# Ten of forty unpacking steps of the first float64 weight chunks, moved from the attention to the routing rounds and behind the branch

## The chip, the cores and the metric

One core of a Trainium2 chip runs the whole program as one launch. The metric is the device time of one execution in microseconds (us): the span from the program's first to its last instruction, and a little around it.

## The reference, cut to what matters

```python
# 1. attention: 2 x 8 heads, 768 positions, head size 64, window 128, 4 sink positions
scores = q @ k.T / sqrt(D);  scores[~(is_sink | in_window)] = -1e9
x = softmax(scores) @ v                      # -> (1536, 512), float32
# 2. routing: every token goes to one of 8 experts, at most 192 tokens to each
logits = x @ w_gate
for idx in argsort(-logits.flatten()):       # greedy, best pair first
    if assigned[tok] < 0 and counts[e] < cap: assigned[tok] = e; counts[e] += 1
# 3. experts: out[mask] = relu(x[mask] @ w1[e]) @ w2[e]
# 4. dense block: h = x @ w_in;  (h * sigmoid(h)) @ w_out
```

`w_in` and `w_out` reach the kernel as float64 (a float32 array times a float64 scalar). All other arrays are float32.

## The kernel before

The work runs in four stages, one after the other, since each needs what the last one leaves.

**Attention** (`attention_band`). The twelve tiles of 128 queries by eight heads give 96 steps `n`, and a loop written out by hand issues all engines' work step by step. At each fourth `n` TensorE makes the scores of four heads (`s_mm`, L271). VectorE takes the merge (`s_merge`, L291) and the masked minimum with its read-out (`s_max`, L299) for each head. ScalarE takes the exponentials two steps later (`s_exp`, L308). TensorE transposes them five steps later (`tr`, L322) and multiplies them with the values thirteen steps later (`pv`, L369, L371, L374). The PSUM pool `s` has four banks, and `s_mm` needs two of them, so it waits until the minima of earlier heads have been read. `hooks[n]` is a list of functions that are called at the top of step `n`, ahead of that step's merge and minimum.

**Unpacking** (`Weights.unpack`). A float64 chunk is loaded as raw 32-bit words into one of seven `raw` buffers (512 KB each) and turned into float32 in `f`. A chunk is four such pieces, and each piece takes five steps: s0 (for the first two chunks ScalarE, an absolute value, L969), s1 (VectorE, clamp, L975), s2 (VectorE, shift and mask, L979), s3 and s4 (VectorE, each combining `raw` and `f`, L983 and L987). Step s4 gives the raw buffer back and issues the load of the next piece. The first two float64 chunks are eight pieces, so forty steps; `unpacked` issues the next one. They are used only in the dense stage.

**Routing** (`Route`). Rounds of threshold tests and counts: VectorE compares (L675 to L692), VectorE and ScalarE build the grids `G` (L710, L715), TensorE counts (L723), VectorE turns the counts into `sel` (L732), TensorE adds it up (L733). Two rounds run over a part of the tiles at the end of the attention (`plan`), four full rounds after it (`run`, `iterate`). `iterate` calls the parts of a round in order: steps, ScalarE's grids, VectorE's grids, counts, rise (`sel` and L733). `between(k)` lets the weights' work run on beside the rounds: ScalarE rounds a float32 piece of an expert's weights (L1014), GpSimd takes the remainder (L1017). Then `finish` makes the row numbers `idx` (L897) and a flag, and a branch on the flag (L778) leads past more rounds that these inputs do not need. GpSimd gathers the first expert pair's rows with three indirect DMAs (L1155).

**Experts and dense block.** TensorE transposes the gathered rows (L1197), ScalarE rounds them (L1211), VectorE takes the remainder (L1212), and the products begin (L1238). All later unpacking is woven between the products.

The `quiet` memsets (L344) are one-element writes on VectorE, 59 of them ahead of the first step.

Of the kernel before, what the change touches and what calls it, by code (L numbers as in the profile page):

```python
# [184 lines left out]
HH = H // 2  # L185
LT, LP, LS = 5, 13, 6
LATE = 9, 10
QUIET = 59
VWS = {8: [((0, (0,)), 0)], 10: [((0, (0,)), 1)], 11: [((0,), 2)], 13: [((0, (1,)), 0)], 16: [((0, (1,)), 1)],
       58: [((1,), 2)]}  # L190
for m in range(1, NT // 2):
# [5 lines left out]
def attention_band(tc, qd, kd, va_d, vt_d, vs_d, sel_d, wbd_d, eye_d, n_sink, ident, x_d, L_sb, pp, hooks={}):  # L197
    nc = tc.nc
    with ExitStack() as ctx:
# [21 lines left out]
        def load_va(i):  # L221
            if i < NT:
                nc.sync.dma_start(va[:, i % NB], va_d[i // NB, i % NB])
# [79 lines left out]
        def s_exp(n):  # L303
            i, h = divmod(n, H)
            if h == 0:
                A[i] = wp.tile([P, H, KW], F32, name="A", bufs=3)
            t, nm = TS.pop(n)
            nc.scalar.activation(A[i][:, h], t, AF.Exp, bias=nm, scale=-1.0)  # L308
            if h == H - 1:
                a = wp.tile([P, 3, H, 4], F32R, name="a96")  # L310
                src = A[i][:, :, 0:4]
                nc.gpsimd.tensor_copy(a[:, 0], src)
                nc.gpsimd.tensor_copy(a[:, 2], src)
                nc.gpsimd.tensor_tensor(a[:, 1], src, a[:, 0].bitcast(F32), OP.subtract)
                A[i, "s"] = a
# [26 lines left out]
        quiet = cp.tile([1, 1], F32, name="quiet")  # L342
        for _ in range(QUIET):
            nc.vector.memset(quiet, 0.0)  # L344
# [3 lines left out]
        def warm(k):  # L348
            for _ in range(k):
                for sl in map(slice, WE, WE[1:]):  # L350
                    nc.tensor.matmul(idle[:, sl], zero[:, :P], zero[:, sl], start=True, stop=True)
# [108 lines left out]
        def feed(*qs):  # L460
            for q in qs:
                if q:
                    f = q.popleft()
                    if f:
                        f()
                    return
# [5 lines left out]
        for n in range(NH + LP + 5):  # L472
            i, h = divmod(n, H)
            now[0] = n
            dve_now.extend(at_step.pop(n, ()))
            if n < NH and n % 4 == 0:
                s_mm(n)
            if n < len(WARM) - 1:
                warm(WARM[n + 1])
            for f in hooks.get(n, ()):  # L480
                if f is None:
                    while dve_now:
                        feed(dve_now)
                else:
                    f()
            if 0 <= n - 2 < NH:
                s_exp(n - 2)
            if 0 <= n - LT < NH:
                tr(n - LT)
            feed(act_now, act_bg)  # L490
            if n < NH and n % 2 == 0:
                s_merge(n)
                s_merge(n + 1)
            feed(dve_now, dve_bg)
            if n < NH:
                s_max(n)
            feed(dve_now, dve_bg)
            feed(act_now, act_bg)
            for _ in range(3 if n >= NH + LT and n - NH not in LATE else 0):
                feed(act_late)  # L500
            it, ht = divmod(n - LS, H)
            if ht == H - 1 and 0 <= it < NT:
                sink_tr(it)
            if n < NH and h == 0:
                if i == 4:
                    nc.sync.dma_start(vsf[1][:96], vs_d[:96, 1])
                if i % 2 == 0:
                    load_vt(i + 2)
                    load_vt(i + 3)
                if i + 3 < NT:  # L510
                    load(i + 3)
                load_va(i + 2)
            for at, f in VWS.get(n, ()):
                (vw, vw_tr, sinks)[f](*at)
            if 0 <= n - LP < NH:
                pv(n - LP)
# [16 lines left out]
NA, RP = 4, 6  # L533
RS, AT = 256.0, (None, 8, None, 9, None, 10, None, 11)
HOT, HOLD = 4, (12, 10, 5, 4)
# [27 lines left out]
class Route:  # L563
# [170 lines left out]
        ]  # L734
        return steps, [partial(grid_act, t) for t in range(na)], grids, counts, rise

    def iterate(self, na, warm=0):
        g = self.G
        parts = self.iteration(NT, na)
        self.warm(warm if g is not None else 0, g)  # L740
        for part in parts:
            for s in part:
                s()

# [4 lines left out]
            s()  # L749
        return oh  # L750

    def run(self, L, idx, nit, more, bg=lambda k: None, speculate=lambda: None):
        self.place(self.psum("s"))
        for k in range(nit):
            bg(k)
            if k + 2 == nit:
                self.foresee("settled")
            self.iterate(NA, HOLD[0] if k == 0 else 0)
            self.warm(HOLD[1 + (k + 1 == nit)])
            if k == 0:  # L760
                self.scaled()
        bg(nit)
        badi = self.result(idx)
        speculate()
        self.warm(HOLD[3])
        self.further(badi, L, idx, more, speculate, "settled")
# [152 lines left out]
SPIN, REST = (2, 2), 9  # L919
MIX, AHEAD = (1, 1, 0), 3  # L920
PLAIN, MIXED = "uuddduuddd", "ududududududu"
FIRST, EVEN, ODD = (17, 25, 33, 45, 53, 60, 67), (40, 46, 52, 58, 64, 70, 76, 80, 84, 88), range(33, 93, 2)


class Weights:
# [631 lines left out]
NIT, MORE, SN = 4, (2, 6), -9  # L1557
# [4 lines left out]
def fused(tc, a, out, n_sink, window):  # L1562
    nc = tc.nc
    with ExitStack() as ctx:
        ctx.enter_context(tc.manual_schedule())
        cp = ctx.enter_context(tc.tile_pool(name="consts", bufs=1))
        dp = ctx.enter_context(tc.tile_pool(name="dram", bufs=1, space=DRAM))
        ident = cp.tile([P, P], F32, name="ident")
        make_identity(nc, ident)
        L = cp.tile([P, NT, E], F32, name="L")  # L1570
        idx = cp.tile([P, E // 2, 3], I32, name="idx")
        x_d = dp.tile([B * S, DM], F32, name="x_d")
        sums_d = dp.tile([NT, P, DM], F32, name="sums_d")
        mix_d = dp.tile([2, P, 3, 4 * 2 * CAP], F32, name="mix_d")
        def load_route():
            route.load(a["offs"], a["dlts"])

        order, mixed = weight_order(a["w1"], a["w2"], a["wi"], a["wo"])
        raws = ctx.enter_context(tc.tile_pool(name="raws", bufs=1, reuse_waits="tile"))
        f64 = ctx.enter_context(tc.tile_pool(name="f64s", bufs=1, reuse_waits="tile"))  # L1580
        W = Weights(tc, raws, f64, order, 4, 7, 4, mixed)
        rest = ExitStack()
        with rest:
            rp = rest.enter_context(tc.tile_pool(name="r_w", bufs=2, side="right"))
            rc = rest.enter_context(tc.tile_pool(name="r_c", bufs=1, side="right"))
            route = Route(tc, rc, ident)
            if banded(n_sink, window):
                pp = rest.enter_context(tc.tile_pool(name="p", bufs=1, space=PSUM))
                hooks = {NT * H // 2: [load_route]}
                for n in FIRST:  # L1590
                    hooks.setdefault(n, []).append(W.load)
                for n in sorted({*EVEN, *ODD}):
                    hooks.setdefault(n, []).append(W.unpacked)
                plan(route, rp, lambda n: pp.tile([P, 512], F32, name=n, bufs=PB[n]), L, hooks)
                attention_band(tc, *(a[k] for k in ("qd", "kd", "va", "vt", "vs", "sel", "wbd", "eye")), n_sink,
                               ident, x_d, L, pp, hooks)
                W.unpack_all()
                route.values(L, NT - 1, NT)
            else:
                load_route()  # L1600
                W.fetch()
                W.unpack_all()
                attention(tc, *(a[k] for k in ("qd", "kd", "vd", "wg")), n_sink, window, ident, x_d, L)
                pp = rest.enter_context(tc.tile_pool(name="p", bufs=1, space=PSUM))
                route.open(rp, lambda n: pp.tile([P, 512], F32, name=n, bufs=PB[n]))
                for s in route.scale(L, NT):
                    s()
                route.begin()
                route.values(L, 0, NT)
            fp = ctx.enter_context(tc.tile_pool(name="ffn", bufs=1, reuse_waits="tile"))  # L1610
            W.start(fp)
            rows = Rows(tc, x_d, idx)
            def between(k):
                if k == NIT:
                    rows.quiet()
                else:
                    W.preload(4, PRE[k])

            route.run(L, idx, NIT, MORE, between, lambda: rows.gather(0))
        W.preload(4)  # L1620
        silu = cp.tile([P, 1], F32, name="silu")
        nc.scalar.activation(silu, ident[:, 0:1], AF.Silu)
        ffn(tc, rows, idx, ident, W, out, sums_d, mix_d)
# [115 lines left out]
```

## Time and profile before

| | us |
|---|---|
| runs | 546.32, 547.36, 548.28 (median 547.36) |
| profiled execution, time | 547.26 |
| profiled execution, span | 545.5 |
| attention, to TensorE's last value product | about 97 |
| full rounds and row numbers, to `idx` | about 122 |
| first product of the experts (L1238) | 128.61 |
| experts to dense block | about 281 |

Times in a profile are counted from the span's start. The profiled execution stands 0.1 us below the median of the runs, and its time is 1.8 us longer than its span.

### The profile page before, as it was taken

How to read it: one execution, taken by the hardware profiler on the slowest of the kernel's cores; microseconds unless marked ns; L12 is line 12 of the kernel's file. 1: busy time of each engine (PE TensorE's matmuls, PEld its weight loads, DVE VectorE, ACT ScalarE, POOL GpSimd, SP SyncE). 2: the span in 40 equal slices, each digit the busy share in tenths (PEclk: the TensorE clock that was granted, in tenths of full speed). 3: DMA queues.
4: the chain of work that ended last, by engine and by line, in shares of the span. 5: the costliest groups of instructions: out<-in, count | busy, mean ns of one | idle time of the engine just before them, and what ended most of it. 6: DMA issues, size and time to landing. Idle time of an engine off the chain costs nothing.

```text
span 545.5 us, 10811 instructions
## 1 busy us (share of the span) xinstructions
PE 526.4 (96%) x3937; PEld 482.4 (88%) x3937; DVE 345.4 (63%) x991; ACT 301.6 (55%) x611; POOL 243.7 (45%) x251
## 2 busy tenths in 40 slices
PE   7999899789999999999999999999999999999995
PEld 6898798667999999999999898998888899888984
DVE  5677898772443453444338998768979877853523
ACT  4677676655776786777644554543554344443330
POOL 4567565377899999999991000000000000000304
PEclk9999999899999999999999999999999999999999
DMA  7989972256466666666640654453677656276503
GB/s 210 381 282 319 316 265 73 76 196 182 143 210 222 223 229 217 226 228 222 225 150 1 258 186 177 172 191 102 220 262 245 234 181 224 99 225 223 194 12 117
DMA packets 43941, 108.00 MB, mean 198 GB/s; under 512 B 4650, under 2 KB 12458, under 8 KB 43884
## 3 DMA queue, kind: packets, MB, share of 16 engines
q1 hardware_dynamic: 41696, 100.88, 54.3%
q0 software_dynamic: 1920, 6.29, 3.4%
q8 instruction: 32, 0.52, 0.4%
q14 instruction: 25, 0.20, 0.1%
q10 hardware_dynamic: 268, 0.10, 0.1%
HBM read 86.81 MB, written 20.45 MB: 197 GB/s over the span
## 4 chain that ended last, share of the span: by engine, by line
PE 69%; issue 4%; POOL 2%; DMA 1%; ACT 0%; DVE 0%; POOLq 0%; another core or an unknown queue 0%; DVEq 0%; ACTq 0%
PE h L1332 21%; PE acc L1454 21%; PE mm L1238 9%; PE m L1261 8%; PE mm L1241 4%; PE m L1264 4%; POOL out L1425 2%; PE mm L1261 1%; PE mm L1197 1%; DMA row<-x_d,idx 1%; PE mm L1264 1%; PE m L1238 0%; POOLq L1735 0%; PE m L1197 0%; ACT wr L1014 0%
## 5 line engine op out<-in xcount | busy, mean ns | idle before, releaser
L1017 POOL TENSOR_TENSOR wr<-raw,wr 128x1024 fp32r<-128x1024 f32 x64 | 150.7, 2390 | 8.2 <-ACT wr L1014 8.1
L1454 PE MATMUL acc<-wr,gt 128*128 128x512 f32 x576 | 145.4, 395 | 0.0
L1454 PEld LDWEIGHTS acc<-wr,gt 128*128 128x128 f32 x576 | 107.3, 188 | 19.4
L1425 POOL DMA_INDIRECT out<-raw,idx x12 | 11.6, 964 | 241.5 <-DVE raw L1466 241.3
L1332 PE MATMUL h<-x,wr 128*128 128x384 f32 x528 | 101.3, 339 | 0.0
L1332 PEld LDWEIGHTS h<-x,wr 128*128 128x128 f32 x528 | 93.8, 188 | 4.0 <-DVE keep L1366 0.3
L1238 PE MATMUL mm<-xg,wr 128*128 128x384 f32 x248 | 72.4, 360 | 0.5 <-DVE xg L1212 0.3
L1014 ACT ACTIVATE wr<-raw 128x1024 fp32r<-128x1024 f32 x64 | 66.8, 1052 | 3.5 <-DMA raw<-in_w 2.1
L1261 PE MATMUL m<-ht,wr 128*128 128x384 f32 x224 | 66.0, 361 | 0.0
L1241 PE MATMUL mm<-xg,wr 128*128 128x192 f32 x248 | 62.1, 250 | 0.0
L1264 PE MATMUL m<-ht,wr 128*128 128x192 f32 x224 | 56.1, 250 | 0.0
L1513 DVE TENSOR_TENSOR gt<-keep,gt 128x384 fp32r<-128x384 f32 x64 | 39.1, 612 | 26.7 <-ACT gt L1319 26.5
L1238 PEld LDWEIGHTS mm<-xg,wr 128*128 128x128 f32 x248 | 46.4, 187 | 1.2 <-DVE xg L1212 0.7
L1241 PEld LDWEIGHTS mm<-xg,wr 128*128 128x128 f32 x248 | 47.3, 191 | 0.0
L1219 DVE TENSOR_TENSOR mm<-mm,t 128x384 f32<-128x384 f32 x33 | 18.7, 567 | 45.0 <-ACT t L1218 45.0
L1318 ACT ACTIVATE keep<-keep 128x384 f32<-128x384 f32 x30 | 15.8, 526 | 54.4 <-DVE keep L1366 54.2
L1264 PEld LDWEIGHTS m<-ht,wr 128*128 128x128 f32 x224 | 42.7, 191 | 0.0
L308 ACT ACTIVATE A<-t,nm 128x132 f32<-128x132 f32 x96 | 35.6, 401 | 11.6 <-DVE nm L299 11.4
L1261 PEld LDWEIGHTS m<-ht,wr 128*128 128x128 f32 x224 | 42.0, 187 | 0.0
L1332 PE MATMUL h<-xn,wr 128*128 128x384 f32 x180 | 36.8, 339 | 0.0
L1332 PEld LDWEIGHTS h<-xn,wr 128*128 128x128 f32 x180 | 32.6, 188 | 2.6
L1319 ACT ACTIVATE gt<-keep 128x384 fp32r<-128x384 f32 x64 | 33.7, 527 | 2.0
(203 smaller groups left out, 934.0 us busy)
## 6 DMA issues: line engine op xcount, KB each, us to landing
raw<-in_w SPq DMA_DIRECT2D x64, 512.0 KB, 4.7
sums_d<-os SPq DMA_DIRECT2D x36, 256.0 KB, 2.0
xn<-mix_d SPq DMA_DIRECT2D x12, 768.0 KB, 4.9
raw<-in_wi SPq DMA_DIRECT2D x16, 512.0 KB, 4.4
raw<-in_wo SPq DMA_DIRECT2D x16, 512.0 KB, 4.7
os<-sums_d SPq DMA_DIRECT2D x24, 256.0 KB, 3.1
mix_d<-xn SPq DMA_DIRECT2D x6, 768.0 KB, 4.1
va<-in_va SPq DMA_DIRECT2D x12, 292.0 KB, 5.9
```

Of the source, the lines that this page charges most:

```text
L308: nc.scalar.activation(A[i][:, h], t, AF.Exp, bias=nm, scale=-1.0)
L1014: nc.scalar.activation(w[:, 0, sl], src(), AF.Copy)
L1017: (nc.vector if k in self.late else nc.gpsimd).tensor_tensor(w[:, 1, sl], src(), w[:, 0, sl].bitcast(F32), OP.subtract)
L1238: nc.tensor.matmul(mm[:, b, :2 * CAP], w[:, 0, fb, d, o:o + P], x[:, d].rearrange("p a t -> p (a t)"), start=d == 0, stop=False, skip_grou ...
L1241: nc.tensor.matmul(mm[:, b, :CAP], w[:, 1, fb, d, o:o + P], x[:, d, 0], start=False, stop=d == 3, skip_group_check=True)
L1261: nc.tensor.matmul(mm[:, d % 2, :2 * CAP], w[:, 0, d // 2, f, o:o + P], ht[:, f].rearrange("p a t -> p (a t)"), start=c == 0 and f == 0, s ...
L1264: nc.tensor.matmul(mm[:, d % 2, :CAP], w[:, 1, d // 2, f, o:o + P], ht[:, f, 0], start=False, stop=last, skip_group_check=True)
L1319: nc.scalar.activation(gt[:, 0], h, AF.Copy)
L1332: nc.tensor.matmul(h, w(a, d), x(b, d), start=start and d == 0 and k == 0, stop=d == n - 1 and k == 2, skip_group_check=True)
L1425: i = nc.gpsimd.indirect_dma_start(out=out, out_offset=bass.IndirectOffsetOnAxis(ap=idx[:, t // 3, t % 3:t % 3 + 1], axis=0), in_=o, in_of ...
L1454: nc.tensor.matmul(a, gt[:, u, ts], w[:, v, 2 * p + i], start=(p, i, k) == (0, 0, 0), stop=(p, i, k) == (1, 1, 2), skip_group_check=True)
L1513: later.popleft()()
```

## The change

Thirty steps are called from the attention's hooks instead of forty: at each odd step from 33 to 83 and at 46, 52, 58 and 64. Two more are called in the first full round, between the counts and the rise. The last eight are called behind the branch, ahead of the rest of the expert weights' first pieces. The memsets on VectorE become 40 ahead of the first step and two at the top of each of the first sixteen steps (72 in place of 59).

```diff
-QUIET = 59
+QUIET, MORE_QUIET, EARLY = 40, 2, 16
@@ attention_band
         for n in range(NH + LP + 5):
             now[0] = n
+            for _ in range(MORE_QUIET if n < EARLY else 0):
+                nc.vector.memset(quiet, 0.0)
@@ Route
-    def iterate(self, na, warm=0):
+    def iterate(self, na, warm=0, aside=None):
-        for part in parts:
+        for k, part in enumerate(parts):
+            if aside and k + 1 == len(parts):
+                aside()
             for s in part:
                 s()
-            self.iterate(NA, HOLD[0] if k == 0 else 0)
+            self.iterate(NA, HOLD[0] if k == 0 else 0, aside if k == 0 else None)
@@
-FIRST, EVEN, ODD = (17, 25, 33, 45, 53, 60, 67), (40, 46, 52, 58, 64, 70, 76, 80, 84, 88), range(33, 93, 2)
+FIRST, EVEN, ODD = (17, 25, 33, 45, 53, 60, 67), (46, 52, 58, 64), range(33, 85, 2)
@@ fused
-                W.unpack_all()
                 route.values(L, NT - 1, NT)
-            route.run(L, idx, NIT, MORE, between, lambda: rows.gather(0))
+            route.run(L, idx, NIT, MORE, between, lambda: rows.gather(0), partial(W.pump, 0, 2))
+        W.unpack_all()
         W.preload(4)
```

## Rows read from the trace of the kernel before

**Rows 1.** TensorE's waits, 18.6 to 128 us (us, times, longest).

```profile
PE s L271 <- DVE nm L299: 1.0, 1, 1.0
PE X L369 <- DVE x L406: 0.4, 1, 0.4
PE s L355 <- DVE rv L419: 0.2, 1, 0.2
```

**Rows 2.** TensorE's waits, 128.7 to 508 us.

```profile
PE mm L1238 <- DVE ht L1223: 0.3, 1, 0.3
```

**Rows 3.** Busy us by stretch: PE, PEld, DVE, ACT, POOL, granted clock, DMA.

```profile
55.50:67.00 11.50, 10.06 (x167) 8.38 (x171) 10.46 (x48) 7.95 (x23) 6.95 (x14) 1.00 0.88 305
67.00:89.00 22.00, 22.00 (x340) 20.21 (x333) 20.28 (x106) 14.30 (x43) 13.80 (x26) 1.00 0.63 219
89.00:99.40 10.40, 7.46 (x79) 6.94 (x79) 8.20 (x36) 7.58 (x25) 3.01 (x7) 1.00 0.13 50
99.90:103.30 3.40, 3.40 (x19) 2.44 (x17) 2.78 (x9) 2.02 (x6) 0.20 (x1) 0.50 0.21 77
```

**Rows 4.** Timeline, VectorE and TensorE, 63 to 67 us (start, us, what, idle before).

```profile
63.92 1.02 DVE L983 SCALAR_TENSOR_TENSOR f<-raw,f 128x512 int32<-128x512 int32 x1
65.08 0.90 DVE L987 SCALAR_TENSOR_TENSOR f<-raw,f 128x512 int32<-128x512 int32 x1
66.80 0.90 PE L271 MATMUL s<-kall,qr 64*64 64x128 f32 x28 [1.01 <-DVE nm L299]
```

**Rows 5.** Groups by form, VectorE, 281 to 480 us (busy us, mean ns).

```profile
L983 DVE SCALAR_TENSOR_TENSOR f<-raw,f 128x512 int32<-128x512 int32 x24 | 16.5, 686 | 0.1
L979 DVE TENSOR_SCALAR f<-f 128x512 int32<-128x512 int32 x24 | 10.1, 421 | 0.1
```

**Rows 6.** Single lines of code, whole span (ns: least, median, most).

```profile
L969 ACT ACTIVATE f<-raw x8: 663/670/682, 31.3 to 78.5; 128x512 f32<-128x512 f32 x8
L314 POOL TENSOR_TENSOR a<-A,a x12: 246/252/762, 12.8 to 92.2; 128x32 fp32r<-128x32 f32 x12
```

**Rows 7.** Timeline, VectorE and GpSimd, 70 to 71 us.

```profile
70.42 0.68 DVE L983 SCALAR_TENSOR_TENSOR f<-raw,f 128x512 int32<-128x512 int32 x1
70.47 0.74 POOL L314 TENSOR_TENSOR a<-A,a 128x32 fp32r<-128x32 f32 x1
```

**Rows 8.** Timeline, all engines, 0 to 19 us.

```profile
1.14 6.65 DVE L344 MEMSET quiet<- 1x1 f32 x59
...
9.15 0.83 PE L322 MATMUL tp<-ident,A 128*128 128x128 f32 x3 [0.83 <-ACT A L308]
...
9.80 0.43 SPq L212 DMA_DIRECT2D qr<-in_qd  x1
...
17.52 0.33 PE L444 MATMUL s<-ident,vwt 128*128 128x128 f32 x1 [0.19 <-DVE nm L299]
```

**Rows 9.** DMA issues of the page (KB each, us to landing).

```profile
qr<-in_qd SPq DMA_DIRECT2D x10, 256.0 KB, 5.8
```

**Rows 10.** Timeline of the first full round.

```profile
102.55 1.99 ACT L1014 ACTIVATE wr<-raw 128x1024 fp32r<-128x1024 f32 x2
...
104.19 0.17 DVE L732 TENSOR_SCALAR sel<-s 128x8 bf16<-128x8 f32 x1 [1.27 <-PE s L723]
```

**Rows 11.** Timeline behind the branch.

```profile
123.09 2.33 PE L1193 MATMUL mm<-wr 128*128 128x512 f32 x9 [0.54 <-DVEq L778]
123.66 0.95 POOL L1155 DMA_INDIRECT row<-x_d,idx  x1 [0.30 <-remote]
...
124.91 0.95 POOL L1155 DMA_INDIRECT row<-x_d,idx  x1 [0.30 <-issue]
...
125.88 4.71 POOL L1017 TENSOR_TENSOR wr<-raw,wr 128x1024 fp32r<-128x1024 f32 x2
...
126.78 0.60 ACT L1211 ACTIVATE xg<-mm 128x512 fp32r<-128x512 f32 x1 [0.74 <-issue]
...
127.41 1.14 DVE L1212 TENSOR_TENSOR xg<-mm,xg 128x512 fp32r<-128x512 f32 x2 [5.53 <-ACT xg L1211]
...
128.61 0.44 PE L1238 MATMUL mm<-xg,wr 128*128 128x384 f32 x1 [0.27 <-DVE xg L1212]
```

More of the change, by code (lines that the diff above doesn't have):

```diff
@@ L750, in settle, with run @@
         return oh
-    def run(self, L, idx, nit, more, bg=lambda k: None, speculate=lambda: None):
+    def run(self, L, idx, nit, more, bg=lambda k: None, speculate=lambda: None, aside=None):
         self.place(self.psum("s"))
```

## The prediction

> **What bounds the kernel now.** I read the chain of waits first: from 128.61 us on it is TensorE's own products. TensorE's waits between 128.7 and 508 us come to a single 0.3 us on VectorE beside the start of the stage itself [rows 2]. So whatever happens after the first expert product keeps its length, and the change is worth what it shifts that product, at 128.61 [rows 11].
>
> Next the table by stretch. From 67 to 89 us TensorE is busy for 22.00 of 22.00 us, while VectorE has 20.28 [rows 3]. Both are nearly full, but TensorE doesn't wait there: taking VectorE work out of that stretch gives nothing by itself. From 55.5 to 67 TensorE has gaps (10.06 of 11.50) and VectorE is the fuller engine. The list of waits says where a gap can be had: 1.0 us at the scores (L271) for a minimum on VectorE, 0.2 at L355 for a reciprocal, and 0.4 at L369 near the end [rows 1]. The timeline shows the first: two unpacking steps, 1.02 and 0.90 us long, stand just ahead of the minimum that frees the bank, and the scores start 1.01 us late [rows 4].
>
> **The attention without ten steps.** With hook 40 gone every later step comes one hook later, and hook 70 is gone too. Counted from hook 61 to the minimum of head 70, VectorE has had s3, s4, s1, s2, s3, s4; it will have s2, s3, s4, s1, s2. The difference is s3 + s4 - s2. Undisturbed that is 0.69 + 0.69 - 0.42 = 0.96 [rows 5]; with the two steps as long as they were there, 1.02 + 0.90 - 0.42 = 1.50 [rows 4]. Either is about TensorE's wait of 1.01. I take 1.0 gained; the lower bound is 0.6 if another step falls into the same company with GpSimd, and the upper is the wait itself. The 0.2 at L355 hangs on the same queue and I take it as gained. The 0.4 at L369 I leave: from the scores of step 92 on, VectorE works on logits and scaling that start when TensorE's products end, with no unpacking among them. What is left of the removal, six steps from 84 on among it, goes into VectorE's idle time beside a full TensorE [rows 3] and is worth nothing.
>
> **The memsets.** Fifty-nine took 6.65 us, 0.113 each [rows 8]. With 42 ahead of the first minimum, that one can start 17 x 0.113 = 1.9 us sooner, and the 0.83 us that TensorE waited at 9.15 for the first exponentials goes. But the queries of the third tile are issued at 9.80 [rows 8] and such a transfer lands 5.8 us later [rows 9], at about 15.6; nothing VectorE does brings them sooner, and the scores of step 16 need them. So most of that is given back. The two memsets at each later step cost 0.23 us of VectorE a step up to step 15, in the stretch where it waits for TensorE. What I keep is the 0.19 us wait at 17.52 [rows 8]: 0.2 gained, between 0 and 0.83 + 0.19 = 1.0.
>
> Sum of the attention: 1.0 + 0.2 + 0.2 = 1.4 us sooner, between 0.2 and 2.0.
>
> **Two steps in the first full round.** s0 goes behind ScalarE's grids, ahead of the two roundings at 102.55: 0.67 us [rows 6], so its result stands at about 103.2. s1 then takes 0.42 [rows 5] to 103.65. `sel` is queued behind it on VectorE and starts at 104.19, after 1.27 us of waiting for the counts [rows 10]. So it costs nothing, and the cover is the slow counting: TensorE's granted clock is 0.50 from 99.9 to 103.3, its lower level of 1.2 GHz, after a stretch in which it was busy for 7.46 of 10.40 us [rows 3]. Were the clock whole, `sel` would be ready sooner and s1 would delay it by at most its 0.42. GpSimd's first remainder slips 0.6 us, and nothing before the branch waits for it.
>
> **Eight steps behind the branch.** They are s2, s3, s4 of one piece, s0 (ScalarE), s1, s2, s3, s4 of the last. In TensorE's row VectorE has passed the branch by about 123.1, and its next work, L1212, waited until 127.41, idle for 5.53 us [rows 11]. The seven VectorE steps are 3 x 0.42 + 4 x 0.69 = 4.0 us, about 4.1 with their starts: 123.1 + 4.1 = 127.2. That fits with 0.2 us to spare, and s0's 0.67 fits into the 0.74 us that ScalarE was idle before 126.78 [rows 11]. Two loads that s4 issues run beside the gathers; I put them at 0 to 0.3 us.
>
> This holds only if nothing stretches those steps, and the rows say that GpSimd does. s3 and s4 read two tiles of SBUF. A GpSimd subtraction that takes 252 ns at the median took up to 762 [rows 6], and the timeline shows why: at 70.47 it met L983 and lasted 0.74 us, to the end of that step [rows 7]. The same company stretched L983 to 1.02 [rows 4]. The two engines shut each other out. Behind the branch stand not such short instructions but the remainders L1017, two in 4.71 us [rows 11], and L1212 is queued behind the last unpacking step.
>
> So the order of arrival decides. On VectorE the last s3 starts at 123.1 + 0.42 + 0.69 + 0.69 + 0.42 + 0.42 = 125.75 and ends near 126.5. The first L1017 is due at 125.88: it waits for s3, then takes its turn of about 2.35 us to 128.8. The last s4 waits, runs 0.69, and ends at 129.5. L1212 starts there in place of 127.41: 2.1 us late, less what overlaps, so I take 2.0. No row of before has L1017 beside such a step; the bounds are 0 (no meeting) and two remainders in the way, 4.7. I take one, because by these starts one step is left when GpSimd comes. The Trainium skill (SBUF — State Buffer, section "SBUF: two separate sides") says that VectorE and GpSimd hold this port pair as an exclusive lock for a whole instruction. The short rows agree with it, and by it one full L1017 would be the wait here.
>
> **Sum.** 547.26 (the profiled execution) - 1.4 + 0 + 2.0 = 547.9, and 0.1 more against the median: 548.0 us. Two runs of this kernel differ by up to 2 us, so less than 0.3% (1.6 us) is no change that can be told.
>
> **Rivals.**
> *VectorE is done before GpSimd comes* (chance 0.30). The gathers are also GpSimd's work. If VectorE's steps hold them up, as they held L314 [rows 7], the gather due at 124.91 ends near 126.5 or later in place of 125.86 and L1017 comes behind it, after s4 has started. Then L1212 waits only for its rows, some 0.4 us late: 547.4 - 1.4 + 0.4 = 546.4. Against it: no row has a gather beside such a step. The Trainium skill (SBUF — State Buffer, same section) warns that DMA descriptors made on GpSimd wait while VectorE uses both ports; by it the gathers would be late as in this rival. No run here shows it.
>
> *Two turns lost* (0.22). If VectorE begins 0.1 us later, L1017 comes while s2 runs and takes the pair ahead of s3; s4 then meets the second L1017. L1212 starts near 127.41 + 4.5, and the time is 547.4 - 1.4 + 4.5 = 550.5; if the gathers take turns as well, 552. This is the case on the slower side, and it decides at a few tenths in the start of the first step behind the branch. For it: the last s3 leads L1017 by only 0.13 us in my count.
>
> *The attention doesn't end sooner* (0.11). TensorE is full from 67 to 89 [rows 3], and if its wait at 66.80 moves to the next group of scores instead of going, 0.2 us is gained and the cost behind the branch stays: 547.4 - 0.2 + 2.0 = 549.2. Against it: the next groups have a full TensorE and fewer steps beside them.
>
> My forecast has 0.37.
>
> **How the numbers follow.** The forecast's own range is 547.2 to 549.4 (attention 0.2 to 2.0, loads 0.3, and about 0.9 us of slow clock either way: the lower level at 99.9 to 103.3 may come again, go, or follow a longer wait behind the branch). Faster than 545.7: about a third of the first rival and little of the forecast, 0.14. Slower than 549.0: nearly all of two turns (0.21), over half of the last rival (0.07) and a fifth of the forecast (0.07): 0.35. The rest, 0.51, is within 0.3%. For 8 in 10 the range runs from 545.6 (0.09 left out below) to 551.0 (0.09 above).
>
> **What would show it.** Right: no wait at the scores near 66 us; `idx` and the gathers some 1.4 us sooner than in [rows 11]; behind the branch one unpacking step (L983 or L987) of 2 to 3 us beside an L1017, with L1212 right behind it, and the first product about 0.6 us later than 128.61. Wrong: all four two-input steps at 0.7 us there, with gathers longer than 0.95 us [rows 11]; or two stretched steps; or a wait for a minimum that turns up at 69 or 72 us. The start would be wrong if TensorE's scores of step 20 came more than 0.5 us earlier than now.

## The result: slower, and the profile after

The changed kernel takes 552.93 us (median of 4 runs, 551.73 to 554.97) against 547.56 (546.32 to 548.28) for the kernel before: ratio 1.010, 95% interval 1.0076 to 1.0123. The prediction was 548.0, range 545.6 to 551.0; the time lies above it. The profiled execution after took 551.73 us with a span of 550.0, 4.5 longer than before. Lines behind the diff have moved by four: L973 is now s0 and L979, L983, L987 and L991 are s1 to s4 (before, L983 was s3), L1159 is a gather, L1021 GpSimd's remainder, L1197 the filler products behind the branch (on weights, while the gathered rows are under way), L1215 the rounding of the gathered rows, L1216 their remainder, L1242 the first product.

TensorE's waits after, 18.6 to 135 us (us, times, longest). The 1.0 at the scores (L271, VectorE) of [rows 1] is gone, and at the top stands a wait that before was 0.27 [rows 11]:

```profile
PE mm L1242 <- DVE xg L1216: 4.5, 1, 4.5
...
PE X L369 <- DVE x L406: 0.4, 1, 0.4
PE s L355 <- DVE rv L419: 0.2, 1, 0.2
```

Timeline: the scores of step 20 and of the group behind the one at 66.80, and the row numbers, before; then the same scores and the first full round after.

```profile
19.00 0.92 PE L271 MATMUL s<-kall,qr 64*64 64x128 f32 x32
...
70.22 0.91 PE L271 MATMUL s<-kall,qr 64*64 64x128 f32 x32
...
121.70 0.18 DVE L897 TENSOR_REDUCE idx<-X 128x12 int32<-128x24 f32 x1 [0.40 <-PE X L880]
```

```profile
18.43 0.43 PE L271 MATMUL s<-kall,qr 64*64 64x128 f32 x7
...
68.55 0.67 PE L271 MATMUL s<-kall,qr 64*64 64x128 f32 x20
...
101.57 0.43 DVE L979 TENSOR_SCALAR f<-f 128x512 f32<-128x512 f32 x1 [0.31 <-ACT f L973]
102.45 0.17 DVE L734 TENSOR_SCALAR sel<-s 128x8 bf16<-128x8 f32 x1 [0.46 <-PE s L725]
```

So 0.57 us was gained by step 20 and 1.67 by the group behind the missing wait. `sel` stands at 102.45 for 104.19 [rows 10], still waiting for the counts with s1 in front of it. The row numbers come 1.88 us sooner (119.82; 121.70 before). Up to there all is gain. Timeline after, behind the branch:

```profile
119.82 0.18 DVE L901 TENSOR_REDUCE idx<-X 128x12 int32<-128x24 f32 x1 [0.40 <-PE X L884]
...
121.21 3.88 PE L1197 MATMUL mm<-wr 128*128 128x512 f32 x9 [0.53 <-DVEq L782]
121.26 0.47 DVE L983 TENSOR_SCALAR f<-f 128x512 int32<-128x512 int32 x1 [1.26 <-DVEq L782]
121.76 0.74 DVE L987 SCALAR_TENSOR_TENSOR f<-raw,f 128x512 int32<-128x512 int32 x1
121.78 0.95 POOL L1159 DMA_INDIRECT row<-x_d,idx  x1 [0.30 <-remote]
122.53 0.69 DVE L991 SCALAR_TENSOR_TENSOR f<-raw,f 128x512 int32<-128x512 int32 x1
123.03 1.01 POOL L1159 DMA_INDIRECT row<-x_d,idx  x1 [0.30 <-issue]
123.14 0.42 DVE L979 TENSOR_SCALAR f<-f 128x512 f32<-128x512 f32 x1
...
123.60 5.46 DVE L983 TENSOR_SCALAR f<-f 128x512 int32<-128x512 int32 x1
124.07 4.69 POOL L1021 TENSOR_TENSOR wr<-raw,wr 128x1024 fp32r<-128x1024 f32 x2
...
125.61 0.60 ACT L1215 ACTIVATE xg<-mm 128x512 fp32r<-128x512 f32 x1 [0.92 <-issue]
...
129.09 0.69 DVE L987 SCALAR_TENSOR_TENSOR f<-raw,f 128x512 int32<-128x512 int32 x1
129.81 0.69 DVE L991 SCALAR_TENSOR_TENSOR f<-raw,f 128x512 int32<-128x512 int32 x1
...
130.42 1.01 DVE L1216 TENSOR_TENSOR xg<-mm,xg 128x512 fp32r<-128x512 f32 x2
131.49 0.48 PE L1242 MATMUL mm<-xg,wr 128*128 128x384 f32 x1 [4.45 <-DVE xg L1216]
```

Read VectorE's lines down: four steps of about their usual length beside the gathers, then s2, a step of 0.42 us, that lasts 5.46, over both remainders of GpSimd (124.07 to 128.76): it is caught. Two steps and L1216 are queued behind it, while L1216's rows are rounded at 126.2. Table by stretch after (busy us of PE, PEld, DVE, ACT, POOL; granted clock; DMA share, GB/s): the clock is at its lower level, 1.2 GHz, twice, under the filler products and again behind the long wait.

```profile
121.50:124.80 3.30, 3.30 (x9) 2.45 (x8) 3.20 (x5) 3.16 (x4) 2.69 (x3) 0.50 0.67 187
126.90:131.40 4.50, 0.14 (x1) 0.00 (x0) 4.43 (x5) 0.00 (x0) 3.96 (x3) 1.00 0.65 206
131.50:135.00 3.50, 3.50 (x14) 3.50 (x15) 0.00 (x0) 0.00 (x0) 0.00 (x0) 0.54 0.91 337
```

The first seven pairs of products (one of L1242 and one of L1245 each) take 3.64 us (131.49 to 135.13). From there to the end it is 414.9 us, and 414.8 from the same product before, so the loss lies between the row numbers and 135 us.

### The profile page after: what moved, and what is told of

It is laid out like the page before. It is cut to its first block, busy times and chain, and to the rows that moved or that the text cites. A ratio compares the mean times of both kernels' runs of the same rounds, so it can differ in the third digit from the quotient of the medians.

```text
span 550.0 us, 10817 instructions
## 1 busy us (share of the span) xinstructions
PE 529.2 (96%) x3937; PEld 485.3 (88%) x3937; DVE 349.8 (64%) x1004; ACT 302.7 (55%) x611; POOL 242.7 (44%) x251
## 4 chain that ended last, share of the span: by engine, by line
PE 84%; issue 5%; DVE 4%; POOL 3%; ACT 2%; DMA 1%; POOLq 0%; DVEq 0%; ACTq 0%
PE h L1336 21%; PE acc L1458 21%; PE mm L1242 9%; PE m L1265 8%; PE mm L1245 4%; PE m L1268 4%; PE s L271 3%; PE X L371 2%; PE X L369 2%; PE tp L322 2%; POOL out L1429 2%; PE mm L1265 1%; PE tp L351 1%; PE tp L911 1%; DMA row<-x_d,idx 1%
## 5 line engine op out<-in xcount | busy, mean ns | idle before, releaser
L1021 POOL TENSOR_TENSOR wr<-raw,wr 128x1024 fp32r<-128x1024 f32 x64 | 150.6, 2387 | 8.3 <-ACT wr L1018 8.2
L1242 PE MATMUL mm<-xg,wr 128*128 128x384 f32 x248 | 74.0, 365 | 4.7 <-DVE xg L1216 4.5
L1245 PE MATMUL mm<-xg,wr 128*128 128x192 f32 x248 | 62.8, 253 | 0.0
L1242 PEld LDWEIGHTS mm<-xg,wr 128*128 128x128 f32 x248 | 47.4, 191 | 5.4 <-DVE xg L1216 4.9
L1223 DVE TENSOR_TENSOR mm<-mm,t 128x384 f32<-128x384 f32 x33 | 18.7, 567 | 46.6 <-ACT t L1222 46.6
L1245 PEld LDWEIGHTS mm<-xg,wr 128*128 128x128 f32 x248 | 48.1, 194 | 0.0
L1222 ACT ACTIVATE t<-mm 128x384 f32<-128x384 f32 x33 | 16.2, 492 | 37.7 <-PE mm L1245 33.9
```

The lines of the kernel that those rows point to most:

```text
L1021: (nc.vector if k in self.late else nc.gpsimd).tensor_tensor(w[:, 1, sl], src(), w[:, 0, sl].bitcast(F32), OP.subtract)
L1223: nc.vector.tensor_tensor(h, h, t, OP.add)
L1242: nc.tensor.matmul(mm[:, b, :2 * CAP], w[:, 0, fb, d, o:o + P], x[:, d].rearrange("p a t -> p (a t)"), start=d == 0, stop=False, skip_grou ...
L1245: nc.tensor.matmul(mm[:, b, :CAP], w[:, 1, fb, d, o:o + P], x[:, d, 0], start=False, stop=d == 3, skip_group_check=True)
```

## Experiments

Each is the changed kernel with one edit, unless said otherwise; each ratio is against the kernel before in the same rounds. "Behind the row numbers" is counted from the start of `idx` in that profile: L1216 started 5.71 us behind them before and 10.60 after, the first product 6.91 and 11.67.

### GpSimd's remainders held until the steps are done

```diff
         W.unpack_all()
+        gate = cp.tile([1, 1], F32, name="gate")
+        nc.vector.memset(gate, 0.0)
+        nc.gpsimd.memset(gate, 0.0)
         W.preload(4)
```

> The changed kernel, with GpSimd's last two remainders held until VectorE's eight steps behind the branch are done (one element that VectorE writes after the last step and GpSimd overwrites before the first remainder). Theory (GpSimd's remainders and VectorE's two-port steps shut each other out, and the long wait then lets TensorE's clock fall): all seven VectorE steps take 0.4 to 0.75 us beside the gathers, the row remainder L1216 starts near 126.3 in place of 130.42, the first product at 126.5 to 127.5 in place of 131.49 and at the whole clock; 546.3 us, some 1.2 below the kernel before and 6 below the changed one. Rival (the loads of the last steps, or the gathers, hold the steps): one step is still some us long without a remainder beside it, and the time stays above 549.

Measured: 546.70 us, ratio 0.9973 (0.9947 to 0.9999). Timeline of this kernel:

```profile
123.32 1.12 POOL L1159 DMA_INDIRECT row<-x_d,idx  x1 [0.30 <-issue]
...
123.89 0.43 DVE L983 TENSOR_SCALAR f<-f 128x512 int32<-128x512 int32 x1
124.35 0.69 DVE L987 SCALAR_TENSOR_TENSOR f<-raw,f 128x512 int32<-128x512 int32 x1
...
125.08 0.69 DVE L991 SCALAR_TENSOR_TENSOR f<-raw,f 128x512 int32<-128x512 int32 x1
...
125.96 2.37 POOL L1021 TENSOR_TENSOR wr<-raw,wr 128x1024 fp32r<-128x1024 f32 x1
...
126.54 1.03 DVE L1216 TENSOR_TENSOR xg<-mm,xg 128x512 fp32r<-128x512 f32 x2 [0.77 <-ACT xg L1215]
...
127.62 0.44 PE L1242 MATMUL mm<-xg,wr 128*128 128x384 f32 x1 [0.27 <-DVE xg L1216]
```

The same s2 at the same place, beside the same gather, takes 0.43 us. VectorE is done at 125.8 and waits 0.77 us for its rows; L1216 then runs beside the remainder without delay (its operand `mm` is in PSUM). The first product comes 7.51 us behind the row numbers in place of 11.67: without the meeting of the step with GpSimd's remainders it is 4.16 us sooner. The theory stands, and the eight steps don't delay L1216, which waits for its rows.

Run again beside a version with the memsets of before:

> The kernel with GpSimd's last two remainders held and the new memsets again, on the chip of the two runs beside it. By its first run 0.9 us below the kernel before: 546.7. If the new memsets bring slow starts on this chip, its median is 0.5 to 1.5 us above that of the one with the old memsets; if they make no difference, both are within 0.3 us.

> The kernel with GpSimd's last two remainders held, and the memsets of before. Theory (the start's slow stretch comes with the new memsets): no slow stretch at 14 us, no 0.57 us gained at the start either, the 1.1 us at the scores near 66 us kept, and 546.5 with fewer runs far above the median. Rival (the memsets make no difference): the same as the kernel with the remainders held and the new memsets, which runs beside it.

Measured: 546.16, ratio 0.9974 (0.9964 to 0.9984), with the new memsets; 546.66, ratio 0.9983 (0.9974 to 0.9992), with the old ones. Both beat both kernels. The medians differ by 0.5 us, neither of the two outcomes written down.

### How a step loses to GpSimd

**Three remainders back to back** (the last one issued twice).

> The changed kernel with the second of GpSimd's two remainders behind the branch issued twice, so that three stand back to back (2.35 us each); the extra one writes the same numbers once more. Theory (VectorE's step gets no turn until GpSimd's chain of remainders ends): the caught step lasts 5.46 + 2.35 = 7.8 us, L1216 starts 10.6 + 2.35 = 13.0 us behind the row numbers in place of 10.6, and the time is 2.4 above the changed kernel, 555.3. Rival (VectorE gets its turn after a fixed wait or after two remainders): the caught step lasts 5.5 us again, one of the two steps behind it (L987, L991) may meet the third, and the time is between 552.9 and 555.3 by where that falls, with a step of about 2.5 to 3 us in the trace.

Measured: 558.20, ratio 1.0174 (1.0138 to 1.0210). Timeline:

```profile
127.94 5.44 DVE L983 TENSOR_SCALAR f<-f 128x512 int32<-128x512 int32 x1
128.41 4.67 POOL L1021 TENSOR_TENSOR wr<-raw,wr 128x1024 fp32r<-128x1024 f32 x2
...
133.16 2.41 POOL L1024 TENSOR_TENSOR wr<-raw,wr 128x1024 fp32r<-128x1024 f32 x1
133.41 2.71 DVE L987 SCALAR_TENSOR_TENSOR f<-raw,f 128x512 int32<-128x512 int32 x1
```

The step got its turn after two remainders, and the third held the next step. But the third writes what the second wrote, and starts 0.08 us after the second's end (128.41 + 4.67 = 133.08); between the first two there is no such gap. L1216 came 12.60 us behind the row numbers, not 13.0. The first theory, no turn until all three end, falls. The median is above both expectations; in this profile the low clock behind the wait lasted for twelve pairs, not seven, and the row numbers came at 124.16, behind loads that were late at the start.

**A third step in the first full round**, so that another step stands where the remainders begin.

```diff
-            route.run(L, idx, NIT, MORE, between, lambda: rows.gather(0), partial(W.pump, 0, 2))
+            route.run(L, idx, NIT, MORE, between, lambda: rows.gather(0), partial(W.pump, 0, 3))
```

> The changed kernel with a third step (s2, L983) in the first full round, so that seven steps are left behind the branch and each comes one place earlier. In all profiles with eight steps the caught one was the same, s2 (one input, 0.42 us alone), 5.4 to 5.5 us long over both remainders; now s3 (L987, two inputs) should start in its place, 0.47 us ahead of the first remainder, and s4 (L991) behind it. Theory (what counts is the order and the kind of the step: a two-input step that stands first runs its 0.7 us, and one that comes second loses one remainder, as in the kernel with three remainders, where s3 took 2.71 us): s3 0.7 to 0.9 us, s4 2.4 to 3.1 us, L1216 about 7.3 us behind the row numbers in place of 10.6 and the first product some 3.3 us sooner at the whole clock; 547.9 us, as the prediction had it. Rival (whichever step is under way when the remainders begin waits for both): s3 or s4 5 us or longer, L1216 10 us or more behind the row numbers, and 552 to 553.

Measured: 553.01, ratio 1.0111 (1.0073 to 1.0150), as the rival has it.

```profile
123.71 5.73 DVE L987 SCALAR_TENSOR_TENSOR f<-raw,f 128x512 int32<-128x512 int32 x1
124.18 4.71 POOL L1021 TENSOR_TENSOR wr<-raw,wr 128x1024 fp32r<-128x1024 f32 x2
```

A two-input step that starts 0.47 us ahead of the first remainder is caught over both as well. The kind of step doesn't matter.

**Only the second remainder held**, and **two one-element memsets between the two**:

```diff
         W.unpack_all()
+        nc.vector.memset(gate, 0.0)
+        W.preload(4, 2)
+        nc.gpsimd.memset(gate, 0.0)
         W.preload(4)
```

In the second kernel `rows.quiet()`, two one-element memsets on GpSimd, stands for the two lines on `gate`, at the place of the lower one.

> The changed kernel with the second of GpSimd's two remainders alone held until VectorE's last step is done; the first follows the gathers as in the changed kernel. Theory (the caught step waits for as many remainders as follow one another without a gap): it lasts 3.0 to 3.2 us in place of 5.46, the two steps behind it 0.7 us each, L1216 starts 8.3 us behind the row numbers in place of 10.6, and the time is 2.3 us or, with TensorE's clock whole at the first products, up to 3.9 below the changed kernel: 549 to 550.6. Rival (the caught step needs two turns of the port pair, one to read and one to write, and loses each to a remainder): with one remainder it loses one, and the same 3.0 to 3.2 us follow here, but nothing is gained by a gap in the run beside it. Second rival (the gather before it is what holds it): 0.4 to 1 us, and 547.

> The changed kernel with two one-element memsets on GpSimd between its two remainders (0.24 us for both elsewhere in the trace). Theory (VectorE gets no turn because the second remainder follows the first without a gap): the caught step ends in or behind the memsets, 3.0 to 3.4 us long, and the next step (s3) or L1216 stands beside or behind the second remainder: s3 2.5 to 2.8 us long if it meets it, and L1216 10 to 10.9 us behind the row numbers. Rival (a gap changes nothing): the caught step lasts 5.7 us, both remainders and the memsets.

Measured: 551.73, ratio 1.0082 (1.0055 to 1.0109), and 552.26, ratio 1.0093 (1.0076 to 1.0110). Timelines of the one and the other:

```profile
125.64 3.14 DVE L983 TENSOR_SCALAR f<-f 128x512 int32<-128x512 int32 x1
126.11 2.38 POOL L1021 TENSOR_TENSOR wr<-raw,wr 128x1024 fp32r<-128x1024 f32 x1
...
130.16 0.68 DVE L1216 TENSOR_TENSOR xg<-mm,xg 128x512 fp32r<-128x512 f32 x1
```

```profile
123.87 3.16 DVE L983 TENSOR_SCALAR f<-f 128x512 int32<-128x512 int32 x1
124.34 2.38 POOL L1021 TENSOR_TENSOR wr<-raw,wr 128x1024 fp32r<-128x1024 f32 x1
...
126.66 0.40 POOL L1153 MEMSET spare<- 1x1 f32 x2
126.90 2.34 POOL L1021 TENSOR_TENSOR wr<-raw,wr 128x1024 fp32r<-128x1024 f32 x1
127.06 2.72 DVE L987 SCALAR_TENSOR_TENSOR f<-raw,f 128x512 int32<-128x512 int32 x1
```

One remainder holds the step for 3.14 us, and L1216 comes 8.32 us behind the row numbers (8.3 expected); the first kernel's time is above the forecast: in its profile the loads came late at the start (row numbers at 121.84), and the seven pairs took 3.63 us. With the memsets between the remainders the step is 2.30 us shorter than over both, and the second remainder then holds the next one. By the records the memsets leave no idle time between the two (126.66 to 127.06 overlaps both), so something else of GpSimd's lets the step in as well as a gap does. What sets the price is how many remainders follow each other with nothing between them: 5.4 to 5.7 us for two, 3.1 to 3.2 for one.

### The low clock behind the long wait

Ten, then eighteen, more filler products behind the transposes, `SPIN = (2, 12)` and `(2, 20)` for `(2, 2)`:

> The changed kernel with ten more warm products of 128x512 on TensorE behind the transposes of the gathered rows, in the stretch where it waits for L1216. Theory (1.6 us of the loss is the first seven product pairs at half the clock, 0.52 us a pair in place of 0.29, because TensorE stood idle for 4.45 us): L1216 still starts near 130.4, but the pairs take 0.29 us from the first on; 1.6 us below the changed kernel, so about 551.3 and 3.8 above the kernel before. Rival (the first products are slow for another reason, such as the transfers under way): the same time as the changed kernel, 552.9.

> The changed kernel with eighteen more warm products of 128x512 on TensorE (ten more left 2.2 us of waiting, and the first product pairs stayed at half the clock). Theory (the clock falls because TensorE stands idle ahead of the first product): with the gap filled to about 0.2 us the pairs take 0.29 us from the first on, and the time is 1.6 us below the changed kernel, 551.3. Rival (the slow pairs come from something other than the idle time): pairs of 0.5 us again, and 553.

Measured: 553.76, ratio 1.0108 (1.0063 to 1.0154), and 553.62, ratio 1.0128 (1.0096 to 1.0160): by the medians nothing is gained. The runs scatter (549.89 to 556.80 for the second), so I go by the profiles, the first product and the table by stretch of the one, then of the other:

```profile
133.53 0.63 PE L1242 MATMUL mm<-xg,wr 128*128 128x384 f32 x1 [2.20 <-DVE xg L1216]
...
133.50:137.00 3.50, 3.46 (x13) 3.47 (x14) 0.00 (x0) 0.00 (x0) 0.00 (x0) 0.52 0.88 303
```

```profile
131.16 0.44 PE L1242 MATMUL mm<-xg,wr 128*128 128x384 f32 x1 [0.39 <-DVE xg L1216]
...
131.20:134.70 3.50, 3.50 (x25) 3.50 (x25) 0.44 (x1) 0.49 (x1) 0.00 (x0) 1.00 0.88 318
```

With 2.20 us of idle time left ahead of the first product the pairs were slow again. With 0.39 left the clock was whole, the seven pairs took 2.08 us (131.16 to 133.24) in place of 3.64, beside about the same transfers (0.88 and 0.91 DMA share), and this execution, 549.89 us, is 1.84 below the changed kernel's profiled one. With the meeting in place the size is shown by that one profile, and the median doesn't bear it out. The profiles of all sixteen kernels side by side agree with it: with 0.27 to 0.39 us of idle time ahead of the first product (nine of them) the seven pairs took 2.08 to 2.10 us, with 2.20 to 6.84 (seven) 3.31 to 3.85.

### The memsets

The kernel before with the new memsets alone, and the changed kernel with the old ones:

> The kernel before with the memsets alone changed (40 ahead of the first step, two at the top of each of the first sixteen). By the prediction 0.2 us sooner from step 20 on. By the trace of the changed kernel, where the scores of step 20 came at 18.43 in place of 19.00, it is 0.57 us: scores of step 20 near 18.45, and 546.9 to 547.0 in the end. Rival: the wait at the scores of step 70 grows by what the start gives (the raw loads come at their own time), and the end stays at 547.4.

> The changed kernel with the memsets of before (59 ahead of the first step, none at the steps). In five of nine profiles of kernels with 40 and two at each step, TensorE's clock was at its lower level for 3.5 to 6.5 us from 14 to 16 us on, behind a wait of 1.3 to 2.6 us for loads that came late; the kernel before shows none in its one profile. Theory (starting sooner leaves TensorE waiting longer for loads that come at their own time, and in part of the executions the clock falls): with the old memsets the runs lie closer together and the median is about 1 us below the changed kernel's, 552, while the meeting behind the branch stays (L1216 10.6 us behind the row numbers). Rival (the late loads and the clock are the chip's, whatever the memsets): the same median and spread as the changed kernel, 553.

Measured: 547.81, ratio 1.0003 (0.9987 to 1.0019), and 552.91, ratio 1.0094 (1.0078 to 1.0109): no difference in the one or the other. The profile of the first was one in which loads came late; its waits and a stretch of its table:

```profile
PE s L454 <- ACT va L447: 1.3, 1, 1.3
PE s L433 <- DMA vt<-in_vt: 0.9, 1, 0.9
```

```profile
14.50:18.00 3.50, 3.50 (x33) 2.63 (x36) 3.27 (x20) 1.98 (x7) 0.66 (x1) 0.50 0.95 310
```

The profiles of six of thirteen kernels with the new memsets have such a start, and none of the three with the old ones. That isn't enough to say that the memsets bring it: run again, the held version with the new memsets had runs as close together as the one with the old.

### Other places for the eight steps

Back to the attention's late hooks, `(46, 52, 58, 64, 76, 80, 84, 88), range(33, 93, 2)`:

> The changed kernel with the eight steps back in the attention, at its late hooks (76, 80, 84, 88 and the odd ones 85 to 91); two stay in the first full round, and only hooks 40 and 70 of before are gone. Theory (the 1.1 us gained at the scores near 66 us come from hooks 40 and 70 alone, and steps beside a full TensorE cost nothing): the scores of the following groups come where they came in the changed kernel (68.55, 71.89, 75.11, 79.21, 83.15), row numbers near 119.9, first product near 126.8; 545.6 us, 1.8 below the kernel before. Rival (one of the later hooks cost something as well, since VectorE is nearly full from 67 to 89): 0.3 to 1 us of the gain is given back there, and a wait for a minimum shows at 70 to 84 us.

Measured: 547.39, ratio 0.9996 (0.9982 to 1.0009). The group behind the missing wait stands at 69.06, 1.16 us sooner than before, with 0.08 of that from the start: the gain at the scores comes without taking steps from the late hooks. The spacing up to 79.72 us is as in the changed kernel, but the next scores, there 3.94 us behind, came 4.59 behind (84.31): a step of 0.68 us at 80.25 stands ahead of a maximum (L632) that TensorE waits for. Its waits:

```profile
PE s L623 <- DVE am L632: 0.3, 1, 0.3
```

The rival holds: a VectorE with room on average still has places where TensorE hangs on it. What was left, row numbers 0.54 us sooner than before, went under slow filler products (first product 7.52 us behind them, 6.91 before).

Behind the first two evacuations of products, four each (`m1(0, 0, late, ops=4)`), and the same with the two steps of the round as well, five each:

> The changed kernel with the eight steps taken from behind the branch and called four each behind the first two evacuations of the experts' products, where VectorE waits for TensorE and GpSimd's two remainders are over. Theory (the eight steps cost something only where a remainder meets them): the first product 7.5 us behind the row numbers, as in the run in which the remainders were held; the steps take 0.4 to 0.75 us each and TensorE doesn't wait for them; 546.7 us, 0.9 below the kernel before. Rival (the two raw buffers that come back some 6 us later, or VectorE late for the next evacuation, cost something): a wait of TensorE for L1223 or for a weight's remainder at 135 to 150 us, and 547.5 or more.

> As the run before it, but with the two steps of the first full round behind the first evacuations as well (five each); the attention still has its thirty steps. TensorE's clock was at its lower level for some 3.5 us just behind the branch in all four profiles with the two steps in the first full round, and in neither of the two without them. Theory (those two steps, by the timing of the round, bring that slow stretch): without them the granted clock is whole from the row numbers to the first product, which comes 6.9 us behind the row numbers as in the kernel before, in place of 7.5; 546.1 us. Rival (the slow stretch has another cause): it is there again, and 546.7.

Measured: 549.39, ratio 1.0043 (1.0025 to 1.0062), and 551.73, ratio 1.0075 (1.0050 to 1.0100). No step is stretched, but they now stand ahead of an evacuation (L1223) and of the second L1216. The first kernel's waits, 128 to 150 us:

```profile
PE mm L1242 <- DVE xg L1216: 2.1, 2, 1.9
```

TensorE waited 1.9 us for that L1216 (2.5 in the second kernel), so VectorE's idle time behind a product was not free. The filler products ran at the whole clock in both profiles (2.32 and 2.33 us), with the two steps in the round and without them, so these steps alone don't bring the low clock; the second kernel's theory falls.

## Why the prediction was wrong

**The account.** Against the profile of before: row numbers 1.88 us sooner; 11.67 - 6.91 = 4.76 lost between them and the first product; 3.64 - 2.08 = 1.56 lost to slow first products. Sum: +4.44, and the spans differ by 4.5. The 4.76 is the meeting's: L1216 starts straight behind the last step, so slower filler products (3.88 us for nine in place of 2.33 [rows 11]) cost nothing beside it. The held kernel's first profile has the slow fillers too, and without the meeting they show: its first product is 7.51 - 6.91 = 0.60 later than before, so holding gave 4.16. In its other profile the fillers took 2.30 us, the first product came 7.05 behind the row numbers, and holding gave 4.62.

**What held.** The length from the first products on is the same, apart from the clock. The wait at the scores went and gave 1.67 - 0.57 = 1.1 (1.0 forecast). The two steps in the full round cost nothing, and a third didn't either. The steps do fit: 121.55 to 125.77 in the held kernel. No gather was lengthened by more than 0.2 us beside two-input steps (0.95 to 1.12 us), so the rival in which GpSimd comes late did not occur. The Trainium skill (SBUF — State Buffer, section "SBUF: two separate sides") lets descriptors made on GpSimd wait while VectorE has both ports; at this size no run here shows it.

**What was slightly off.** The start gave 0.57 in the profile for 0.2, by the prediction's own test more than it allowed. In the seven profiles with the new memsets and no late loads it is 0.08 to 0.75, and the three comparisons of medians give it between -0.2 and 0.5. The 0.2 at L355 stayed. Behind the group at 68.55 another 1.88 - 1.67 = 0.21 came, which the prediction had at nothing.

**The step that failed** is "it waits for s3, then takes its turn of about 2.35 us", one remainder for one step: L1216 was to start 2.0 us late for its rows, and was 4.2 late. Two things in it were wrong. First, the step that was under way did not hold GpSimd off: s2 started 0.47 us ahead of the first remainder's record, longer than the 0.43 it takes when GpSimd is held, and was still caught. Second, VectorE got no turn between the two remainders, which follow each other with nothing between them. The count of starts was short as well: in the held kernel the last s3 starts 4.24 us behind the row numbers (124.35 less 120.11), not 4.05, so that s2 stood there when GpSimd came, which is the condition of the rival "two turns lost". But a start ahead of GpSimd would not have saved s3 either: with three steps in the round it stood 0.47 us ahead and was caught. That rival had the size, 4.5, but as two steps losing one turn each; its 550.5 lacks the slow clock. The Trainium skill (SBUF — State Buffer, section "SBUF: two separate sides") says that where a VectorE operation needs the port pair that it shares with GpSimd, whichever of the two engines starts first keeps the pair for its whole instruction. That a whole remainder is waited for agrees (with one, the step ends at 128.78, 0.29 us behind it); by the recorded starts the caught first-comer doesn't, and the two remainders in a row aren't in that sentence. The runs decide.

**The second term** was the clock. The prediction put 0.9 us on it either way and only into the range; a wait of 4.45 us ahead of full work cost 1.6 by itself.

Open: why a step that starts 0.47 us ahead is caught (the remainder may hold the ports before its recorded start; GpSimd's records are rough). In all eight profiles with a meeting the caught step leads by 0.47 or 0.48 us, so no run shows how early a step has to start to get through. Why the clock falls at 121 us in some profiles and not in others is open too: the held kernel had it in one profile and not in the other. The median of the runs after lies 1.2 us above its profiled execution, the fastest of the four. The profile of the changed kernel with the old memsets, at 553.06, has the same stretch behind the row numbers (first product 11.66 behind them, seven pairs 3.64) and row numbers at 120.99, 1.17 later; whether the other three runs after differ in the same place isn't shown.

## What to carry to other kernels

Before moving VectorE steps between SBUF tiles into an idle stretch, look at what GpSimd runs there: a step that met GpSimd subtractions with nothing between them waited for all of them, here 5.0 us for two, and everything queued behind it waited too. Hold the GpSimd work if it isn't urgent (one element written by VectorE and overwritten by GpSimd was enough); that version is 0.27 and 0.26% faster than the kernel before in its two runs. Count the slow products behind a long wait of TensorE as a term of its own.

## What the runs showed that was not expected

- A gap of 0.08 us between two GpSimd subtractions let a waiting VectorE step through, and so did two one-element memsets between them; with nothing between, the step waited for 4.7 us of them.
- L1216, with an operand in PSUM, started beside a remainder at once, as at 126.54 in the held kernel, while steps between SBUF tiles were shut out.
- With 0.39 us of idle time ahead of it TensorE's first product ran at 2.4 GHz; after 2.20 and 4.45 us the first seven pairs ran at 1.2 GHz.
